# A gated linear attention with a mixture of experts on one core: one GpSimd drain is added in the last expert's first layer

## The chip, the cores and the metric

The kernel runs on one core of one Trainium2 chip. The time is the device time of one execution in microseconds; lower is better.

## What is computed

The attention part keeps a 48 x 48 state for each of 4 batches and 8 heads and steps it through 768 tokens; its output, 3072 tokens of 384 numbers, is the input of a mixture of eight experts, of which each token uses one:

```python
for t in range(S):
    state = alpha[:, :, t, :, None] * state + np.einsum('bhd,bhe->bhde', k[:, :, t], v[:, :, t])
    y[:, :, t] = np.einsum('bhd,bhde->bhe', q[:, :, t], state)
...
    h = np.maximum(x[b, s] @ w1[e], 0.0)
    out[b, s] = p[e] * (h @ w2[e])
```

The expert `e` of a token is the argmax of eight logits, or the expert of the token before it where a second gate says so; `p[e]` is the softmax weight. The inner width of an expert is 1024.

## The kernel before

The program first computes the attention in 24 blocks of 128 tokens (batch by batch within each slice of time). Beside it, routing builds for every expert a list of its tokens. The first expert is worked off in two jobs, `a` and `b`, partly beside the attention. The other seven experts are ordered by their number of tokens, and each is a job of its own, `r0` to `r6`, with as many tiles of tokens as its rank is given in `RANKS` (the last one, `r6`, has 128 + 128 + 112 rows).

A job has these steps. `gather` (line 237) fetches the rows of its tokens from DRAM with one indirect DMA on GpSimd for each tile. `trans` (line 248) transposes them on TensorE and splits them into a high and a low part. `gemm1` (line 261), the first layer, goes through eight slices `f` of the inner width: nine matmuls each into one of three PSUM tiles (`halves`, line 868), then a relu on ScalarE into `hh` and a subtraction on VectorE into `hl`. `gemm2` (line 284), the second layer, makes 24 matmuls for each tile of tokens. `store` (line 324) scales the result by the softmax weight on VectorE and sends it to its places in the output with an indirect DMA on GpSimd.

The main loop is `for n, j in enumerate(jobs)` at line 1073, with `nx` the job behind `j`. During `gemm1` of a job, GpSimd gathers the rows of `nx`, and weights of this job and the next are split by `piece` (line 1077): ScalarE makes the high part, VectorE the low part, GpSimd that of one w1 piece of a rank. In the last job, `r6`, there is no `nx`: nothing is gathered, and only the pieces 5 and 6 of its own weights, of w2, are split at `f` = 0 and 1, on ScalarE and VectorE.

The order of the instructions on each engine is the written one: every call of an engine goes through a wrapper (`Engine`, line 87, `call` at line 96) that pins it behind the call before it. Therefore nearly all rows of the profile carry line 97, the wrapper's. SyncE's queue loads the inputs and weights; GpSimd's queue has the gathers, the stores, and some elementwise work of the attention.

Behind the loop stands a branch for overflow, `with tc.If(NT > 0)` at line 1146 (`NT` is loaded at line 1144): tokens that did not fit into the tiles of their rank. With these inputs it is not taken, and each engine runs only the events that close it. Line 1303 is the line at which the program's closing barrier is made, line 1300 that of its opening one; both contain a DRAIN on every engine.

Of the kernel before, what the change touches and what calls it, by code (L numbers as in the profile page):

```python
# [72 lines left out]
def gla_moe(ctx, tc, akq, vw, vn, wg, w1, w2, cst, tok, out):  # L73
# [30 lines left out]
    v_, s_, g_, t_, y_ = (Engine(e) for e in (nc.vector, nc.scalar, nc.gpsimd, nc.tensor, nc.sync))  # L104
# [31 lines left out]
    def cc(k, p0=0, p1=128):  # L136
        a, b = _off[k]
        return cs[p0:p1, a:b]
# [928 lines left out]
    def spread(k, n):  # L1067
        return [(t + 1) * n // (k + 1) for t in range(k)]
# [4 lines left out]
    for n, j in enumerate(jobs):  # L1073
        nx = jobs[n + 1] if n + 1 < len(jobs) else None
        W, Wn = Ws[n], Ws[n + 1] if nx else None

        def piece(w, p):
            w.split(p)
            if len(w.raw) < 7:
                w.load()  # L1080
            elif n + 2 < len(Ws) and w is Wn:
                Ws[n + 2].load()
            elif Wn is not None and w is W:
                Wn.load()

        if nx:
            if n:
                nx.numbers()
            gt = nx.gather()
        for f, _ in enumerate(j.gemm1(W)):  # L1090
            if n == 1 and f == 4:
                nt = mp.tile([8, 1], F32, bufs=1, name="nt")
                gr = mp.tile([8, NOV], F32, bufs=1, name="gr")
                v_.tensor_tensor(gr, cntp.broadcast_to([8, NOV]), cc("jt", 0, 8), ALU.is_gt)
                v_.tensor_reduce(nt, gr, AX.X, ALU.add)
            if n and f < 2:
                piece(W, 5 + f)
            if n == 0 and f == 1:
                ct = pp.tile([8, 2, 128], F32, tag="xp", name="ct")
                t_.transpose(ct[:, 0], rest[:, 0], ident)  # L1100
                t_.transpose(ct[:, 1], rest[:, 1], ident)
                v_.tensor_copy(capp, ct[:, 0, 0:1])
                v_.scalar_tensor_tensor(cntp, ct[:, 1, 0:1], HALF, cc("base", 0, 8), ALU.add, ALU.subtract)
            if n == 0 and f == 2:
                for put in kept:
                    put()
            if nx:
                if 1 <= f:
                    next(gt, None)
                if n and f in (3, 5, 7):  # L1110
                    piece(Wn, (f - 3) // 2)
                if n == 0 and f % 2:
                    piece(Wn, f // 2)
            if j.thin and 2 <= f < 6:
                W.again(f - 2)
        if n == 1:
            pc.close()
            qp = ctx.enter_context(tc.tile_pool(name="qp", bufs=1, space=PSUM))

            def whole(j):  # L1120
                return lambda s, P=None: qp.tile([P or j.ways[s].stop - j.ways[s].start, DM], F32, tag="yp", bufs=3, name=f"yp_{j.nm}_{s}")
            for m in jobs[1:]:
                m.y, m.tpt = whole(m), ((pp, "xp"), (qp, "tp"))
        at_ = spread(nx.ns, 4 * j.ns - 3 * j.thin) if nx else []
        tr = nx.trans() if nx else None
        for q, _ in enumerate(j.gemm2(W)):
            if n == 1 and q == 3:
                tp = qp.tile([8, 2], F32, tag="tp", name="ovt")
                t_.matmul(tp[:, 0:1], lhsT=cc("tri8", 0, 8), rhs=nt, start=True, stop=True)
                t_.matmul(tp[:, 1:2], lhsT=cc("ones", 0, 8)[:, 0:8], rhs=nt, start=True, stop=True)  # L1130
                cum = mp.tile([8, 2], F32, bufs=1, name="cum")
                v_.tensor_copy(cum, tp)
                ti = mp.tile([8, 1], I32, bufs=1, name="ti")
                v_.tensor_copy(ti, cum[:, 1:2])
            if nx and q == 2 or nx and n and q == 0:
                piece(Wn, 3 + q // 2)
            for _ in range(at_.count(q)):
                next(tr)
        for _ in tr or ():
            pass  # L1140
# [166 lines left out]
```

## Time and profile before

| what | value |
|---|---|
| runs | 394.98, 393.0, 394.84 us, median 394.84 us |
| profiled execution | 392.89 us, span 391.1 us |
| instructions | 11445 |
| mean granted clock | 0.992 |
| TensorE busy | 95% of the span |
| VectorE, ScalarE, GpSimd busy | 64%, 45%, 43% |

The span goes from the first to the last instruction of the core. The time of an execution also holds what lies around the span, 1.8 us here. The busy times count only what an engine itself executes; waiting, branching, semaphore events and drains are done by the engine's sequencer (written with a q behind the engine's name) and are not counted.

### The profile page before, as it was taken

To read this page: it belongs to the slowest core of one execution; us is meant where nothing else is said; L and a number is where in the kernel's file an instruction comes from. 1 tells how busy PE (TensorE), PEld (TensorE's weight loads), DVE (VectorE), ACT (ScalarE), POOL (GpSimd) and SP (SyncE) were. 2 spreads that over 40 slices of the span, in tenths; PEclk is the share of its full clock that TensorE was granted. 3 is DMA by queue.
4 is the path that set the end of the run, shared out by engine and by line. 5 is a ranking of instruction groups with operands and counts; after the bars stand their busy time and mean duration, and the time that the engine had idled before them with its cause. 6 is when DMAs were issued, how large, how long until landed. Compare 5 with 4: busy or idle time off the path is not lost.

```text
span 391.1 us, 11445 instructions
## 1 busy us (share of the span) xinstructions
PE 370.5 (95%) x4536; PEld 340.9 (87%) x4536; DVE 248.5 (64%) x565; ACT 177.9 (45%) x452; POOL 166.4 (43%) x226
## 2 busy tenths in 40 slices
PE   7989988989999999999999999999999999999990
PEld 7878877878878899998899899999899899999990
DVE  8999989999875476755643562554554764564310
ACT  2476767787766530534521541542362461643200
POOL 7559666756677123344323612532522432612020
PEclk9999999999999999999999999999999999999996
DMA  8998899876746101784451572484286274561010
GB/s 235 230 246 218 234 265 261 255 208 187 208 116 180 41 2 38 226 273 151 134 163 45 153 224 78 129 293 176 100 255 251 74 236 134 158 189 59 1 42 7
DMA packets 27002, 63.30 MB, mean 162 GB/s; under 512 B 4964, under 2 KB 11446, under 8 KB 26946
## 3 DMA queue, kind: packets, MB, share of 16 engines
q1 hardware_dynamic: 23218, 52.37, 46.3%
q0 software_dynamic: 3584, 10.04, 7.4%
q8 instruction: 36, 0.59, 0.6%
q14 instruction: 20, 0.16, 0.1%
q10 hardware_dynamic: 144, 0.14, 0.1%
HBM read 53.09 MB, written 10.04 MB: 161 GB/s over the span
## 4 chain that ended last, share of the span: by engine, by line
PE 64%; DVE 15%; issue 12%; DMA 3%; POOL 2%; ACT 2%; SPq 0%; DVEq 0%; POOLq 0%; ACTq 0%
PE h_r L97 20%; PE yp_r L97 19%; PE py L97 5%; DVE sf L97 4%; DVE A L97 4%; PE pz L97 3%; DMA ld<-akq 2%; PE yp_b L97 2%; PE tp_r L97 2%; PE up L97 2%; PE h_a L97 2%; DVE pq L97 2%; POOL out L97 2%; PE yp_a L97 1%; DVE st L97 1%
## 5 line engine op out<-in xcount | busy, mean ns | idle before, releaser
L97 POOL DMA_INDIRECT out<-yo_r,ix_r x25 | 24.9, 996 | 123.4 <-DVE yo_r L97 99.1
L97 PE MATMUL yp_r<-w2h_r,hh_r 128*128 128x384 f32 (+2 forms) x184 | 63.5, 345 | 0.0
L97 PE MATMUL yp_r<-w2h_r,hl_r 128*128 128x384 f32 (+2 forms) x184 | 61.8, 336 | 0.0
L97 PE MATMUL yp_r<-w2l_r,hh_r 128*128 128x384 f32 (+2 forms) x184 | 61.6, 335 | 0.0
L97 PE MATMUL h_r<-xh_r,w1h_r 128*128 128x384 f32 (+5 forms) x168 | 59.6, 355 | 0.0
L97 PE MATMUL h_r<-xl_r,w1h_r 128*128 128x384 f32 (+5 forms) x168 | 59.4, 354 | 0.0
L97 PE MATMUL h_r<-xh_r,w1l_r 128*128 128x384 f32 (+5 forms) x168 | 59.3, 353 | 0.0
L97 DVE SCALAR_TENSOR_TENSOR hl_r<-h_r,hh_r 128x384 fp32r<-128x384 f32 (+3 forms) x56 | 32.8, 585 | 39.5 <-ACT hh_r L97 39.0
L97 ACT ACTIVATE hh_r<-h_r 128x384 fp32r<-128x384 f32 (+3 forms) x56 | 28.7, 513 | 42.8 <-PE h_r L97 42.6
L97 DVE TENSOR_TENSOR_SCAN sf<-ld,sf,zp 112x128 f32<-112x128 f32 x96 | 38.3, 462 | 0.9
L97 PEld LDWEIGHTS yp_r<-w2h_r,hh_r 128*128 128x128 f32 (+2 forms) x184 | 34.1, 186 | 0.3
L97 PEld LDWEIGHTS yp_r<-w2l_r,hh_r 128*128 128x128 f32 (+2 forms) x184 | 34.2, 186 | 0.3
L97 POOL TENSOR_TENSOR ld<-ld,sf 112x512 f32<-112x512 f32 x24 | 28.4, 1183 | 13.9 <-DVE sf L97 13.3
L97 PEld LDWEIGHTS yp_r<-w2h_r,hl_r 128*128 128x128 f32 (+2 forms) x184 | 34.1, 185 | 0.2
L97 PEld LDWEIGHTS h_r<-xh_r,w1h_r 128*128 128x128 f32 x168 | 31.5, 188 | 3.0 <-issue 1.2
L97 POOL TENSOR_TENSOR ld<-ld,A 112x512 f32<-112x512 f32 x24 | 28.4, 1183 | 13.4 <-DVE A L97 7.3
L97 PEld LDWEIGHTS h_r<-xl_r,w1h_r 128*128 128x128 f32 x168 | 31.5, 188 | 2.1 <-DVE xl_r L97 0.3
L97 PEld LDWEIGHTS h_r<-xh_r,w1l_r 128*128 128x128 f32 x168 | 31.5, 188 | 1.8
L97 ACT CAST xh_r<-tp_r 128x384 fp32r<-128x384 f32 (+4 forms) x25 | 11.4, 456 | 47.0 <-PE tp_r L97 45.9
L97 DVE TENSOR_TENSOR_SCAN A<-ld,zp 112x260 f32<-112x260 f32 x48 | 30.8, 683 | 2.7
L97 POOL DMA_INDIRECT xg_r<-xd,ix_r x25 | 28.7, 1148 | 8.6 <-issue 5.7
L97 DVE TENSOR_TENSOR xl_r<-tp_r,xh_r 128x384 fp32r<-128x384 f32 (+4 forms) x25 | 13.1, 525 | 28.1 <-ACT xh_r L97 28.1
(217 smaller groups left out, 778.6 us busy)
## 6 DMA issues: line engine op xcount, KB each, us to landing
rw_r<-w SPq DMA_DIRECT2D x21, 512.0 KB, 4.0
rw_r<-w SPq DMA_DIRECT2D x28, 384.0 KB, 4.3
ld<-akq SPq DMA_DIRECT2D x44, 192.0 KB, 4.7
vt<-vn SPq DMA_DIRECT2D x24, 192.0 KB, 4.0
xd<-XR SPq DMA_DIRECT2D x24, 192.0 KB, 3.9
ld<-akq SPq DMA_DIRECT2D x44, 97.7 KB, 4.5
wf_r<-w SPq DMA_DIRECT2D x8, 384.0 KB, 5.1
rw_a<-w SPq DMA_DIRECT2D x3, 512.0 KB, 5.0
```

The costliest lines, as they stand in the source:

```text
L97: r = f(*a, **k)
```

## The change

A call of `drain` on GpSimd is added to the main loop. It is made once, in the last job (`not nx`), when the second slice (`f == 1`) of its first layer has been written. It goes through the same wrapper as the other calls, so on GpSimd it stands behind the last store of `r5` and ahead of the first store of `r6`.

```diff
@@ -1095,6 +1095,8 @@
                 v_.tensor_reduce(nt, gr, AX.X, ALU.add)
             if n and f < 2:
                 piece(W, 5 + f)
+            if not nx and f == 1:
+                g_.drain()
             if n == 0 and f == 1:
                 ct = pp.tile([8, 2, 128], F32, tag="xp", name="ct")
                 t_.transpose(ct[:, 0], rest[:, 0], ident)
```

## Rows read from the trace of the kernel before

**Rows 1.** The page: span, and TensorE's busy time, share and instructions.
```profile
span 391.1 us, 11445 instructions
...
PE 370.5 (95%) x4536; PEld 340.9 (87%) x4536; DVE 248.5 (64%) x565; ACT 177.9 (45%) x452; POOL 166.4 (43%) x226
```

**Rows 2.** Windows: busy us of each engine from the last matmul to the end.
```profile
core 0: us, PE busy (x) PEld busy (x) DVE busy (x) ACT busy (x) POOL busy (x), PEclk, DMA share, GB/s
381.40:391.10 9.70, 0.33 (x2) 0.00 (x0) 0.62 (x1) 0.00 (x0) 0.96 (x1) 0.67 0.02 7
```

**Rows 3.** Timeline of GpSimd, last stores: start, us, what, idle before and its releaser.
```profile
358.14 0.98 POOL L97 DMA_INDIRECT out<-yo_r,ix_r  x1 [3.47 <-DVE yo_r L97]
374.33 0.98 POOL L97 DMA_INDIRECT out<-yo_r,ix_r  x1 [15.21 <-DVE yo_r L97]
378.50 0.98 POOL L97 DMA_INDIRECT out<-yo_r,ix_r  x1 [3.18 <-DVE yo_r L97]
382.66 0.96 POOL L97 DMA_INDIRECT out<-yo_r,ix_r  x1 [3.18 <-DVE yo_r L97]
```

**Rows 4.** Timeline of all engines, from 381 us on.
```profile
381.39 0.34 PE L97 MATMUL yp_r<-w2h_r,hl_r 128*112 128x384 f32 x1
381.77 0.62 DVE L97 TENSOR_SCALAR yo_r<-yp_r,pr 112x384 f32<-112x384 f32 x1 [3.54 <-PE yp_r L97]
```

**Rows 5.** Source line 1146, GpSimd: duration in ns (min/median/max), first and last start.
```profile
L1146 POOLq INC_SWDGE_SEM  x1: 1354/1354/1354, 384.1 to 384.1; - x1
```

**Rows 6.** Source line 1303: GpSimd and SyncE, whole and in windows around 385.4, 386 and 390.3.
```profile
L1303 POOLq DRAIN  x3: 46/107/4811, 385.4 to 390.8; - x3
L1303 DVEq DRAIN  x2: 10/14/17, 383.2 to 390.5; - x2
...
L1303 POOLq DRAIN  x1: 4811/4811/4811, 385.4 to 385.4; - x1
...
L1303 SPq EVENT_SEMAPHORE  x12: 28/28/28, 385.4 to 386.0; - x12
L1303 SPq DRAIN  x2: 7/10/13, 386.1 to 386.2; - x2
...
L1303 POOLq EVENT_SEMAPHORE  x2: 17/17/17, 390.3 to 390.4; - x2
```

**Rows 7.** DMA issues of GpSimd (xcount, median us to landing); packets after 384.9 us.
```profile
xg_r<-xd,ix_r POOLq DMA_INDIRECT x25, 4.3
out<-yo_r,ix_r POOLq DMA_INDIRECT x25, 2.6
...
xg_a<-xd,ix_a POOLq DMA_INDIRECT x2, 3.3
xg_b<-xd,ix_b POOLq DMA_INDIRECT x2, 3.0
out<-yo_a,ix_a POOLq DMA_INDIRECT x2, 4.4
out<-yo_b,ix_b POOLq DMA_INDIRECT x2, 3.7
...
DMA packets 0, 0.00 MB, mean 0 GB/s; under 512 B 0, under 2 KB 0, under 8 KB 0
```

**Rows 8.** Source line 1300, GpSimd: the drain of the opening barrier.
```profile
L1300 POOLq DRAIN  x1: 178/178/178, 0.3 to 0.3; - x1
```

**Rows 9.** Timelines of GpSimd, VectorE and TensorE: a subtraction beside GpSimd, and the last job's.
```profile
339.06 2.40 POOL L97 TENSOR_TENSOR w1l_r<-rw_r,w1h_r 128x1024 fp32r<-128x1024 f32 x1 [1.62 <-issue]
...
339.58 0.56 DVE L97 SCALAR_TENSOR_TENSOR hl_r<-h_r,hh_r 128x384 fp32r<-128x384 f32 x1 [1.00 <-ACT hh_r L97]
...
359.27 0.54 DVE L97 SCALAR_TENSOR_TENSOR hl_r<-h_r,hh_r 128x368 fp32r<-128x368 f32 x1 [1.41 <-ACT hh_r L97]
...
361.56 0.33 PE L97 MATMUL h_r<-xh_r,w1h_r 128*128 128x368 f32 x1
```

## The prediction, made before the changed kernel ran

> **What bounds the kernel now.** I read the page's engine shares first, then the windows, then GpSimd's timeline, and last the sequencer rows of the lines that close the program, because the shares alone do not show where this change acts. TensorE is busy for 370.5 us of a 391.1 us span [rows 1], so almost everywhere time is set by matmuls. The exception is the end: from 381.4 to 391.1 us, 9.7 us, TensorE works 0.33 us, VectorE 0.62 and GpSimd 0.96 [rows 2]. The last matmul begins at 381.39 us, VectorE scales the result at 381.77, GpSimd issues the last store at 382.66 and is done issuing at 383.62 [rows 3, 4]. The remaining 7.5 us hold no engine work at all; they belong to sequencers, which the busy rows leave out.
>
> What fills them can be read from the lines that close the overflow branch and the program. GpSimd's sequencer runs an INC_SWDGE_SEM of 1.354 us from 384.1 [rows 5], then a DRAIN from 385.4 that lasts 4.811 us, and only at 390.3 the two semaphore events with which it releases the other engines [rows 6]. SyncE has meanwhile waited through twelve events, from 385.4 to 386.0, and its own DRAIN of the closing barrier stands at 386.2 [rows 6]. VectorE's first drain of that line stands at 383.2 [rows 6], and TensorE and ScalarE have been done for longer. So from 386.2 to 390.3 everybody waits for one GpSimd drain.
>
> Is that drain waiting for data? The store issued at 382.66 takes about 2.6 us to land (the median of its kind) [rows 7], which gives 385.3, and after 384.9 no DMA packet moves at all [rows 7]. The drain starts after that. It is therefore busy with something other than the transfer. Its two neighbours are the clue: the same line shows three GpSimd drains of 46, 107 and 4811 ns [rows 6], and the one at the program's start took 178 ns [rows 8]. The long one is the only one with GpSimd's DMAs behind it: 25 + 25 + 2 + 2 + 2 + 2 = 58 indirect DMAs [rows 7], gathers and stores. 4811 / 58 = 83 ns for each. I read it as a walk over every GpSimd DMA since the last drain, landed or not; this is a reading of four numbers, not something the trace shows directly.
>
> **The change, part by part.** One instruction is added to GpSimd's stream, in the written order, after the last store of rank 5 and ahead of the first store of rank 6. Nothing is removed or moved, and SP's queue is untouched.
>
> *The new drain itself.* The store ahead of it is issued from 358.14 to 359.12 us, the first one behind it at 374.33 [rows 3]. Landing of the store ahead: 358.14 + 2.6 = 360.7 us. Its price is unknown; the nearest rows are 0.046 us (a drain with nothing to do) and 4.811 us (one over 58 DMAs) [rows 6]. I take 55 x 0.083 = 4.6 us, nearest to the second, since 55 of the 58 DMAs are older than it. If the walk begins only after landing it ends at 360.7 + 4.6 = 365.3 us; GpSimd is then idle for 9 more us. The cover is GpSimd's idle time of 15.21 us before 374.33 [rows 3]; if it were gone, the whole 4.6 us would delay rank 6's first store, and so the ones behind it. Queued behind the drain are only the three stores and the closing sequence; no other engine waits for GpSimd there, because the last rank has no gathers and its two late weight splits run on ScalarE and VectorE. Cost on the path: 0.
>
> *The closing drain.* It now has three DMAs behind it instead of 58: 3 x 0.083 = 0.25 us, in place of 4.81. Bounds: 0.046 us and 4.811 us. I add the 0.178 us of the start's drain as a base [rows 8], 0.43 us in all, so it would end at 385.4 + 0.4 = 385.9.
>
> *What is late next.* Not GpSimd any more but SyncE, whose drain stands at 386.2 [rows 6]. Its twelve waits begin when INC_SWDGE_SEM ends, 384.1 + 1.35 = 385.4, and that one ends with the last store's landing, which the change does not move. So GpSimd's event moves from 390.3 to 386.2: a gain of 4.1 us, not of the drain's 4.4.
>
> The sum: 0 - 4.1 us. Against the profiled execution, 392.89 us with a span of 391.1, that is 388.8. The three runs shown have a median of 394.84, 1.95 us above the profiled one, although their lowest, 393.0, lies close to it; I carry the difference over: 394.84 - 4.1 = **390.7 us**, 1.0% faster.
>
> **One rule weighed.** All drains of SyncE and the 46 ns one of GpSimd are short; GpSimd's at 385.4 is four hundred times longer than SyncE's median of 10 ns [rows 6]. The Trainium skill, VectorE: DVE Perf Modes, section "The DRAIN you can't avoid", says that the drains of a program's preamble and postamble take a constant 12 ns or so on all five engines. By that the added drain would cost nothing and give nothing, and the sum would be 394.8 us. The 4811 ns row contradicts it for GpSimd.
>
> **The rivals.**
> - *The closing drain's length is its own* (chance 0.11). It may be a fixed price of the first drain after DMA work, or a drain may not shorten the list that the next one walks. Then nothing changes: 394.8 us. For it: only one long drain is on record, so no scaling is shown. Against it: of the two drains of the same line that follow, neither is over 107 ns, so a drain does leave the next one little to do. To this rival belongs an added drain that skips GpSimd's DMAs. The page's rule above gives the same time.
> - *Only part is given back* (0.07). If older DMAs are dropped from the list on the way, as others reuse their places, the 4.8 us belong to fewer DMAs and the last three weigh more. With a list of 10, each costs 0.48 us and three cost 1.44: the drain would end at 385.4 + 1.44 = 386.9, a gain of 3.4 us, 391.4 us. With 6 left, 2.4 us: the gain is 2.4 and the time 392.4.
> - *VectorE is held up* (0.04), the slower side. If the drain keeps VectorE off SBUF while it walks, the place is hl of the last rank's first layer, due at 359.27 for 0.54 us [rows 9]. Three PSUM tiles serve h, so the fourth group of nine matmuls, at 361.56, waits for that hl to be done [rows 9]: 361.56 - 359.81 = 1.75 us of slack. A hold until 359.2 + 4.6 = 363.8 ends hl at 364.3, 2.8 us late on TensorE. If the closing drain stays long, the sum is 394.84 + 2.8 = 397.6 us. Against it: a real GpSimd operation of 2.40 us at 339.06 runs across an hl that starts at 339.58 and still takes 0.56 us [rows 9]. The Trainium skill, SBUF — State Buffer, section "Who interferes with whom", has an exclusive lock between GpSimd and VectorE only for VectorE instructions with two SBUF inputs or in a two-port mode; the hl row, with one input from PSUM, agrees.
>
> **How the numbers follow.** The forecast has a chance of 0.78, the rivals 0.11, 0.07 and 0.04. About 0.5%, 2.0 us here, can be told from no change. Faster by more: the forecast and the partial case, 0.85. Same: the first rival, 0.11. Slower: 0.04. The range starts at the lowest of the runs shown less the sum, 393.0 - 4.1 = 388.9, less another 0.4 for closing events that shift with the shorter drain: 388.5. It reaches up over the partial case with six DMAs to 392.5, and leaves out no change and slower, 0.15 together, and what the partial case has above that.
>
> **What would show it.** In the changed profile a GpSimd DRAIN of the kernel's wrapper line should stand between 359 and 366 us with about 4.6 us, GpSimd's stores of rank 6 at the same distance from the last matmuls as now, and the closing drain well under 1 us, with the span at about 387.0. A closing drain still near 4.8 us proves the first rival; one between 1 and 3 us the second; hh or hl rows that slide past 361.56 the third. If the closing drain is short and the end still comes late, SyncE's twelve events or the INC_SWDGE_SEM have grown, and the step "late next" is the wrong one.

## The result and the profile after

The changed kernel took 389.95, 389.84, 390.67 and 388.01 us, median 389.89, beside a median of 393.92 us for four runs of the kernel before. The ratio of the changed kernel to the one before is 0.9854 (95% interval 0.981 to 0.9898); it is not formed from these two medians, whose quotient is 0.990. In a second series with more runs the ratio is 0.9905 (0.9874 to 0.9937). The two intervals overlap from 0.9874 to 0.9898; the kernel is faster by about 1%, as forecast (390.7 us, range 388.5 to 392.5).

The profiled execution took 389.95 us with a span of 388.1. The second of these windows of the kernel after, from its last matmul on, answers to [rows 2], GpSimd's timeline to [rows 3], the timeline of all engines to [rows 4]; the first window is that of the added drain:

```profile
core 0: us, PE busy (x) PEld busy (x) DVE busy (x) ACT busy (x) POOL busy (x), PEclk, DMA share, GB/s
...
359.00:365.00 6.00, 6.00 (x38) 6.00 (x37) 3.45 (x7) 3.36 (x6) 0.98 (x1) 1.00 0.07 27
382.60:388.10 5.50, 0.36 (x3) 0.02 (x1) 0.62 (x1) 0.00 (x0) 0.96 (x1) 0.91 0.04 12
...
359.36 0.98 POOL L97 DMA_INDIRECT out<-yo_r,ix_r  x1 [3.47 <-DVE yo_r L97]
375.56 0.98 POOL L97 DMA_INDIRECT out<-yo_r,ix_r  x1 [15.21 <-DVE yo_r L97]
379.73 0.98 POOL L97 DMA_INDIRECT out<-yo_r,ix_r  x1 [3.18 <-DVE yo_r L97]
383.89 0.96 POOL L97 DMA_INDIRECT out<-yo_r,ix_r  x1 [3.17 <-DVE yo_r L97]
...
382.62 0.34 PE L97 MATMUL yp_r<-w2h_r,hl_r 128*112 128x384 f32 x1
383.00 0.62 DVE L97 TENSOR_SCALAR yo_r<-yp_r,pr 112x384 f32<-112x384 f32 x1 [3.54 <-PE yp_r L97]
```

Up to the last store nothing is nearer or farther than before: the store still comes 1.27 us after the last matmul's start (382.62 to 383.89; before 381.39 to 382.66), and GpSimd's idle time ahead of rank 6's stores is 15.21, 3.18 and 3.17 us, within 0.01 us of [rows 3]. What shrank is the part behind: from the last store's start to the end of the span 388.1 - 383.9 = 4.2 us, before 391.1 - 382.7 = 8.4 us. The span fell by only 3.0 us, because this execution reached its last matmul 1.2 us later than the one profiled before; it is already 0.9 us later at the first gather of job `a`, at 115.9 us instead of 115.0, more than 200 us ahead of the added drain, and the whole 1.2 us later at the store just ahead of that drain (359.36 against 358.14). That is the scatter of the body from one execution to the next, not the change.

The sequencer rows of the kernel after (lines 97, 1148 and 1305 answer to the wrapper's line 97 and to lines 1146 and 1303 of before) show where the 4.2 us went; the last line is the time that the last store took to land:

```profile
L97 POOLq DRAIN  x1: 5790/5790/5790, 359.1 to 359.1; - x1
...
L1148 POOLq INC_SWDGE_SEM  x1: 254/254/254, 385.3 to 385.3; - x1
...
L1305 POOLq DRAIN  x3: 46/107/1146, 385.6 to 387.8; - x3
...
L1305 SPq EVENT_SEMAPHORE  x12: 28/28/961, 385.5 to 387.1; - x12
L1305 SPq DRAIN  x2: 7/10/13, 387.2 to 387.2; - x2
...
L1305 POOLq EVENT_SEMAPHORE  x2: 17/17/17, 387.3 to 387.3; - x2
...
DMA to landing us min/median/max: 2.7/2.7/2.7
```

Four things stand in these rows. The added drain stands on the sequencer from 359.1 to 364.9 us, and the issue of the store ahead of it (359.36 to 360.35) lies inside that row, so behind the issue it takes 4.57 us; TensorE is busy throughout (6.00 of 6 us from 359 to 365). The closing drain fell from 4811 to 1146 ns. INC_SWDGE_SEM, an instruction of GpSimd's sequencer in the closing of the overflow branch, fell from 1354 to 254 ns, which the prediction had not expected. And one of SyncE's twelve events, all of 28 ns before, now takes 961 ns and ends at 386.6: SyncE waits there for the landing of the last store (383.9 + 2.7). GpSimd's releasing events follow SyncE's drain, 387.3 after 387.2; GpSimd's own drain ended at 385.6 + 1.1 = 386.7.

### The profile page after: what moved, and what is told of

The parts are those of the page before. It is cut to its first block, busy times and chain, and to the rows that moved or that the text cites. A ratio compares the mean times of both kernels' runs of the same rounds, so it can differ in the third digit from the quotient of the medians.

```text
span 388.1 us, 11446 instructions
## 1 busy us (share of the span) xinstructions
PE 371.4 (96%) x4536; PEld 341.8 (88%) x4536; DVE 248.7 (64%) x565; ACT 178.0 (46%) x452; POOL 166.7 (43%) x226
## 4 chain that ended last, share of the span: by engine, by line
PE 62%; DVE 16%; issue 14%; DMA 3%; POOL 2%; ACT 1%; POOLq 0%; DVEq 0%; SPq 0%; ACTq 0%
PE h_r L97 20%; PE yp_r L97 20%; DVE sf L97 5%; DVE A L97 4%; PE py L97 4%; PE pz L97 4%; PE h_a L97 2%; PE tp_r L97 2%; PE up L97 2%; DVE pq L97 2%; DVE st L97 2%; PE yp_a L97 1%; POOL out L97 1%; DMA xg_r<-xd,ix_r 1%; PE lq L97 1%
```

## The experiments

**The changed kernel again.** No edit; more rounds.

> The changed kernel itself, timed in more rounds. The closing part, from the start of the last store to the end of the span, took 8.4 us before and 4.2 us after in the two profiles, so the theory that the whole gain is the shorter closing drain (walk theory: about 83 ns for each GpSimd DMA since the last GpSimd drain) expects 4.0 to 4.4 us less than the kernel before, a ratio of 0.989 to 0.990. A second gain somewhere in the body, which the ratio of 0.985 with its interval of 0.981 to 0.990 leaves room for, would show as a ratio below 0.987.

Measured: ratio 0.9905 (0.9874 to 0.9937), median 390.03 against 394.9 us. The medians are 4.9 us apart, the ratio stands for 3.8 us, and the 4.2 us of the closing part lie between. From the last store to the end of the span it took 4.1 us. The interval holds the gain of the closing part, about 4.2 / 394.9 = 1.1%, and the ratio gives no sign of a second one. Why the first series gave 0.985 is not shown; its own medians give 0.990.

**The drain where nothing hides it.**

```diff
+    g_.drain()
     pinned[0] = False
     NT = nc.values_load(...
```

(without the call in the loop)

> The same drain, but written behind the last store of the last rank, so that nothing hides it. Walk theory: it visits all 58 DMAs where it stands, 58 x 83 ns = 4.8 us from 383.6, and the closing drain then only waits for nothing or little (under 0.3 us); the span ends within 0.5 us of the kernel before, 391 us. Rival (an added drain makes the closing one cheap at no price of its own): about 4 us faster, as the change was.

Sequencer rows of this kernel, the added drain, INC_SWDGE_SEM, the closing drains, and the load of `NT` on GpSimd; the last line is the same load in the kernel before:

```profile
L97 POOLq DRAIN  x1: 6008/6008/6008, 382.8 to 382.8; - x1
...
L1147 POOLq INC_SWDGE_SEM  x1: 195/195/195, 390.5 to 390.5; - x1
...
L1304 POOLq DRAIN  x3: 34/51/107, 390.7 to 392.0; - x3
...
L1145 POOLq TENSOR_LOAD <-ti x1: 503/503/503, 389.3 to 389.3; - x1
...
L1144 POOLq TENSOR_LOAD <-ti x1: 505/505/505, 382.8 to 382.8; - x1
```

The last store is issued from 383.06 to 384.02 and the drain ends at 388.8, 4.8 us behind it. The first of the closing drains, the one that took 4811 ns before, takes 51 ns. The time is that of the kernel before, 0.9985 (0.9958 to 1.0011). The span, though, ended at 392.3 us and not within 0.5 us of 391: its part behind the last store took 9.2 us, 0.8 more than before. The load of `NT` and the branch, which GpSimd's sequencer ran beside the last store before, wait for the drain here. So a drain does not make the work cheaper, it does it earlier; the change gains because it does it beside matmuls.

**A drain of another engine.**

```diff
             if not nx and f == 1:
-                g_.drain()
+                v_.drain()
```

> The added drain is one of VectorE at the same place of the program, none of GpSimd. Walk theory: nothing changes, the closing GpSimd drain stays at 4.7 to 4.9 us and the ratio is 0.997 to 1.003. Rival (any added instruction shifts what follows, such as the loading of code, and the gain comes from that): a ratio near 0.99.

```profile
L97 DVEq DRAIN  x1: 997/997/997, 361.8 to 361.8; - x1
...
L1305 POOLq DRAIN  x1: 4811/4811/4811, 385.8 to 385.8; - x1
```

Ratio 1.0006 (0.9974 to 1.0039), and the closing GpSimd drain has the very 4811 ns of [rows 6]. (The 997 ns of VectorE's drain hold the 0.96 us split of w2 that begins with it.) This shifts the code of VectorE alone, not GpSimd's; that a shift of GpSimd's code is not the cause either is shown further on, where the same GpSimd drain, put elsewhere, leaves closing drains of 1605 and 3483 ns.

**The drain where its cover is short.**

```diff
         for q, _ in enumerate(j.gemm2(W)):
+            if not nx and q == 8:
+                g_.drain()
```

(without the call in `gemm1`)

> The GpSimd drain stands between the second and the third store of the last rank, where GpSimd has about 3.2 us to spare. Walk theory: it visits 57 DMAs, 57 x 83 ns = 4.7 us from the end of the second store's issue (379.5 us in the profile before), so until 384.2; the last store, otherwise at 382.7, starts some 1.7 us later, and the end is 1.7 us later than in the changed kernel: a gain of some 2.5 us, a ratio of 0.993 to 0.995. Rival (an added drain is free wherever it stands): a gain of 4 us.

GpSimd's and VectorE's timelines of this kernel, last tile, and its closing rows:

```profile
382.85 0.98 POOL L97 DMA_INDIRECT out<-yo_r,ix_r  x1 [3.18 <-DVE yo_r L97]
389.47 0.96 POOL L97 DMA_INDIRECT out<-yo_r,ix_r  x1 [5.64 <-issue]
...
386.12 0.62 DVE L97 TENSOR_SCALAR yo_r<-yp_r,pr 112x384 f32<-112x384 f32 x1 [3.54 <-PE yp_r L97]
...
L1148 POOLq INC_SWDGE_SEM  x1: 209/209/209, 390.9 to 390.9; - x1
...
L1305 POOLq DRAIN  x1: 1061/1061/1061, 391.1 to 391.1; - x1
```

The ratio is 0.9929 (0.9897 to 0.9961): the gain is smaller than with the drain in its cover, though the intervals of the two overlap. The trace is clearer. The drain's row (5950 ns from 382.6) ends at 388.6, 4.7 us behind the second store's issue. The last store's data were ready at 386.74, and without the drain the store would have begun 0.27 us later, as in [rows 3, 4]: 387.0. It begins at 389.47, 2.5 us late, where 1.7 were expected; behind the drain's end 0.9 us more go by until the issue begins, which the walk does not include. So by the trace the gain left is 8.4 - (2.5 + 4.1) = 1.8 us, with the 4.1 us behind the last store, and not the expected 2.5; the ratio stands for 2.8. This profiled execution is one of the long ones of its series (395.41 us, median 391.86), in part for what is told at the end.

**Another number of DMAs on the list.** In two kernels the only drain stands earlier, in a third the kernel before has more DMAs:

```diff
+            if n == 4 and f == 7:
+                g_.drain()
...
+            if n == 1 and f == 7:
+                g_.drain()
...
+            if n and f > 4:
+                g_.dma_start(scr[:, 3 * (n - 1) + f - 5], cst[0:16, 0:4])
```

> The drain is moved to the last slice of the first layer of the fourth ranked expert; 39 GpSimd DMAs stand ahead of it and 19 behind. Walk theory (83 ns for each DMA since the last GpSimd drain): 39 x 83 ns = 3.2 us there; the closing drain takes 19 x 83 ns = 1.6 us, and INC_SWDGE_SEM, which fell from 1.354 us with 58 DMAs to 0.254 with 3 and 0.195 with none, takes 0.195 + 19 x 0.020 = 0.58 us. Rival (the first drain behind DMA work pays a fixed price of 4.7 us): 4.7 us in the middle, and the closing one ends with the landing of the last store, about 1.1 us, as in the changed kernel.

> The drain is moved to the last slice of the first layer of the first ranked expert; 16 GpSimd DMAs stand ahead of it and 42 behind. Walk theory: closing drain 42 x 83 ns = 3.5 us, INC_SWDGE_SEM 0.195 + 42 x 0.020 = 1.04 us. Fixed-price rival: a closing drain of about 1.1 us and INC_SWDGE_SEM of 0.25 us.

> The kernel before, without any added drain, and with 21 more GpSimd DMAs that carry 256 bytes each (three in each ranked expert's first layer, into a scratch tile that nothing reads). Walk theory by DMAs: the closing drain goes through 79 instead of 58, 79 x 83 ns = 6.6 us, and INC_SWDGE_SEM takes 0.195 + 79 x 0.020 = 1.8 us. Rival (the walk is over rows or bytes): the closing drain stays at 4.8 to 4.9 us. Fixed-price rival: 4.8 us.

Closing rows of the three kernels, in this order; for the first also the added drain and the GpSimd work ahead of it:

```profile
285.84 2.39 POOL L97 TENSOR_TENSOR w1l_r<-rw_r,w1h_r 128x1024 fp32r<-128x1024 f32 x1 [1.83 <-ACT w1h_r L97]
...
L97 POOLq DRAIN  x1: 5718/5718/5718, 285.8 to 285.8; - x1
...
L1148 POOLq INC_SWDGE_SEM  x1: 574/574/574, 385.0 to 385.0; - x1
...
L1305 POOLq DRAIN  x1: 1605/1605/1605, 385.6 to 385.6; - x1
```

```profile
L1148 POOLq INC_SWDGE_SEM  x1: 1034/1034/1034, 385.3 to 385.3; - x1
...
L1305 POOLq DRAIN  x1: 3483/3483/3483, 386.4 to 386.4; - x1
```

```profile
L1149 POOLq INC_SWDGE_SEM  x1: 1801/1801/1801, 385.5 to 385.5; - x1
...
L1306 POOLq DRAIN  x3: 46/103/6526, 387.3 to 394.4; - x3
```

Put in order of the GpSimd DMAs issued since the last GpSimd drain:

| kernel | DMAs | INC_SWDGE_SEM, ns | closing drain, ns |
|---|---|---|---|
| drain behind the last store | 0 | 195 | 51 |
| drain before the last store | 1 | 209 | 1061, waits for the landing |
| changed kernel | 3 | 254 | 1146, waits for the landing |
| drain in the fourth ranked expert | 19 | 574 | 1605 |
| drain in the first ranked expert | 42 | 1034 | 3483 |
| kernel before | 58 | 1354 | 4811 |
| kernel before, 21 small DMAs more | 79 | 1801 | 6526 |

Where the drain does not wait for a landing, it is a straight line: (6526 - 1605) / 60 = 82 ns for each DMA, 83 to 84 from zero. The added drain of the fourth ranked expert fits as well: with 39 DMAs it ended at 291.5 us, 3.3 us behind the work ahead of it (285.84 + 2.39 = 288.23), where the walk wanted 3.2 and a fixed price 4.7. INC_SWDGE_SEM follows another: (1801 - 195) / 79 = 20 ns for each. The small DMAs carry 256 bytes each, the others up to 192 KB; the price goes by DMAs, not by bytes or rows. A fixed price of the first drain is excluded. In the one execution of each kernel the spans were 388.0 (19 DMAs), 390.7 (42) and 394.7 us (79).

**Is the list cleared?** The drain of the fourth ranked expert and that of the change together, and the same with the first one in the fifth ranked expert:

```diff
+            if (n == 4 and f == 7) or (not nx and f == 1):
+                g_.drain()
...
+            if (n == 5 and f == 7) or (not nx and f == 1):
+                g_.drain()
```

> Both drains: the one of the fourth ranked expert and the one of the change. Walk theory: the second finds 16 DMAs, 16 x 83 ns = 1.3 us behind the end of the last issue, so it ends with the landing of that store, about 1.6 us behind its issue, where it ended 4.57 us behind it in the changed kernel; the closing drain is as in the changed kernel. Rival (a drain goes through all GpSimd DMAs of the program again): the second still ends 4.6 us behind the issue.

The second drain ended 2.2 us behind the issue (3413 ns from 363.3, the issue ending at 364.53). That is far from the 4.6 us of a walk over everything, so a drain clears the list for the next one; but the walk theory, as written, wanted 1.6. The store landed at 366.0, 2.5 us after its start, and the drain ended 0.7 us behind that. In the closing drains with 3 DMAs and with 1 the same distance was 0.17 and 0.08 us. A second theory, two passes of 41 ns for each DMA with the wait between them, was put against a single pass:

> As the run with two drains, but the first stands in the fifth ranked expert, so that the second finds 9 DMAs. There the second drain ended 0.70 us behind the landing of the store ahead of it with 16 DMAs on the list, and the closing ones 0.17 us behind it with 3 and 0.08 with 1. Two-pass theory (each pass 41 ns for a DMA; the first passes over the list and waits for the last landing, the second follows it): 9 x 41 ns = 0.37 us and 0.04, so 0.4 us behind the landing. One-pass theory (83 ns each, then the wait for the last one): 0.1 us behind the landing, and the 0.70 us was a disturbance.

> The run with two drains once more. Two-pass theory: the second drain ends 0.65 to 0.75 us behind the landing again. One-pass theory: 0.1 us behind it.

The second drain of either kernel and the store ahead of it, first with 9 DMAs, then with 16 again:

```profile
L97 POOLq DRAIN  x1: 3126/3126/3126, 359.7 to 359.7; - x1
...
359.89 0.99 POOL L97 DMA_INDIRECT out<-yo_r,ix_r  x1 [3.47 <-DVE yo_r L97]
```

```profile
L97 POOLq DRAIN  x1: 3412/3412/3412, 362.3 to 362.3; - x1
...
362.52 0.98 POOL L97 DMA_INDIRECT out<-yo_r,ix_r  x1 [3.47 <-DVE yo_r L97]
```

With 2.5 us to landing, the first landed at 362.4 and the drain ended at 362.8, 0.4 us behind it; the second at 365.0 and 365.7, 0.7 us behind it again. Four points, 0.08, 0.17, 0.4 and 0.7 us for 1, 3, 9 and 16 DMAs, lie on one line of some 41 ns for each, from 0.04 us. A fifth point was on record already: the added drain of the first ranked expert, with 16 DMAs, ended 0.71 us behind the landing of the newest. About half of the 83 ns is paid only when the newest DMA has landed. That there are two passes is the simplest reading; the rows do not show the passes themselves.

**What the end waits for now.** The last tile's scaling was divided between two engines, in the changed kernel:

```diff
-            v_.tensor_scalar_mul(yo, yp, self.pr[0:P, 0, s:s + 1])
+            c = DM // 2 if self.nm == "r6" and s == 2 else DM
+            v_.tensor_scalar_mul(yo[:, 0:c], yp[:, 0:c], self.pr[0:P, 0, s:s + 1])
+            if c < DM:
+                s_.mul(yo[:, c:], yp[:, c:], self.pr[0:P, 0, s:s + 1])
```

> The changed kernel with the last tile's scaling divided: VectorE makes the left 192 columns, ScalarE the right 192, which shortens the way from the last matmul to the last store. If the landing of the last store is what the end now waits for, the time from the end of the last matmul to the end of the span falls by what the store moves forward, about 0.25 us, from 5.0 to 5.1 us to 4.75 to 4.85. If the closing drain's own walk or INC_SWDGE_SEM still set the end, it falls by the same, since these follow the store too, but the closing drain would be longer than the wait for the landing; if something else of the program's end does, it stays at 5.0 to 5.1.

```profile
388.82 0.42 DVE L97 TENSOR_SCALAR yo_r<-yp_r,pr 112x192 f32<-112x192 f32 x1 [3.54 <-PE yp_r L97]
389.27 0.42 ACT L97 ACTIVATE yo_r<-yp_r,pr 112x192 f32<-112x192 f32 x1 [12.49 <-DVE yo_r L97]
389.96 0.96 POOL L97 DMA_INDIRECT out<-yo_r,ix_r  x1 [3.43 <-ACT yo_r L97]
```

A miss: the halves share a tile, so ScalarE waited for VectorE, and they ran one behind the other; a half also costs 0.42 us, not half of 0.62. From the last matmul to the end it took 5.2 us instead of 5.0 to 5.1. The store came 0.25 us later relative to the last matmul, and the part behind it stayed at 4.0 to 4.1 us, so the end does follow the last store. The other traces tell more: in the seven executions with one or three DMAs on the closing list, the last store lands 2.54 to 2.71 us after its start, and the span ends 1.50 us behind the landing in every one. So the end waits for that landing. A version that beats the changed kernel did not come out of this.

## What the prediction had right, and the step that failed

*The long drain is a walk over GpSimd's DMAs.* Right, and its 83 ns too: 82 ns from the slope between 19 and 79 DMAs, with a row of 51 ns for none. "Landed or not" is right of the first half of the price alone: some 41 ns of it for each DMA are due only behind the newest landing.

*The added drain, 55 x 0.083 = 4.6 us, hidden.* Right: 4.57 us behind the store's issue, ended at 364.9, and GpSimd's wait of 15.21 us ahead of the next store has not changed by a hundredth. That the walk might begin only after landing is refuted: it would have ended 4.6 us behind the landing and ended 3.1 behind it.

*The closing drain, 0.43 us.* Mis-sized: it took 1.146 us. The term had three DMAs and a base, and left out that a drain with a store in flight waits for its landing; before, the landing was over when the drain began. It cost nothing on the path, since GpSimd's drain ended at 386.7 and SyncE's came at 387.2.

*INC_SWDGE_SEM ends with the last store's landing, which the change does not move.* This is the step that failed. In the profile before it ended at 385.4, just behind the landing at 385.2, and I took nearness for a cause. The runs show 20 ns for each DMA on the list plus 0.195 us: 1.354 us with 58, 0.254 with 3. In the changed kernel it ends at 385.5, 1.0 us ahead of the landing at 386.6. So the change did move this term, and SyncE's twelve events with it.

*SyncE is late next.* Right, for another reason. Its twelve events do begin when INC_SWDGE_SEM ends, now 1.1 us earlier relative to the last store, but one of them then stands 961 ns for the landing. The two differences nearly cancel: SyncE's drain came 3.5 us behind the last store's start before (386.2 - 382.7) and 3.3 us after (387.2 - 383.9). Hence 4.2 us from the closing part where the sum said 4.1. That they cancel is luck: with 58 DMAs INC_SWDGE_SEM happens to end 2.75 us behind the last store's start, and the landing comes after 2.6 to 2.7 us.

*From the sum to the time.* 390.7 forecast, 389.89 measured. The sum was set on a median of 394.84, 1.95 us above the profiled execution; with one run more the median of before is 393.92, and 393.92 - 4.1 = 389.8. By these runs the base was off, by the scatter of single executions; in the second series it is 394.9 again, with 390.03 for the changed kernel. Times do not settle here where the last 0.8 us lie.

*The signs.* The prediction said that a closing drain between 1 and 3 us would prove the partial case. It took 1.146 us, and yet the partial case is wrong: the sign did not reckon with the wait for the landing. The span was to be at about 387.0 and was 388.1, for the 1.2 us of scatter in the body.

*The rivals.* A fixed price of the closing drain fell with the table above. So did, for GpSimd, the rule of the Trainium skill, VectorE: DVE Perf Modes, section "The DRAIN you can't avoid", that such drains take some 12 ns on every engine; on the other four engines the closing drains took 7 to 17 ns, as it says. (GpSimd's is 481 times SyncE's median, not four hundred.) The partial case fell as well: the price for each DMA is the same with 19 and with 79 on the list, so none of the 58 had been dropped on the way. VectorE was not held up:

```profile
360.50 0.54 DVE L97 SCALAR_TENSOR_TENSOR hl_r<-h_r,hh_r 128x368 fp32r<-128x368 f32 x1 [1.41 <-ACT hh_r L97]
361.21 0.96 DVE L97 TENSOR_TENSOR w2l_r<-rw_r,w2h_r 128x768 fp32r<-128x768 f32 x1 [0.18 <-ACT w2h_r L97]
...
362.78 0.33 PE L97 MATMUL h_r<-xh_r,w1h_r 128*128 128x368 f32 x1
```

These rows of the kernel after stand inside the added drain. The subtraction takes the 0.54 us of [rows 9] and begins with the same wait for ScalarE; the fourth group of matmuls begins 2.28 us after it, before 361.56 - 359.27 = 2.29. Even the split of w2, with two inputs in SBUF, takes 0.96 us, as in the kernel before.

## What to carry to other kernels

Look at what the sequencers do behind the last engine work; the busy rows do not show it, and a closing GpSimd drain there cost 83 ns in this kernel for every DMA that GpSimd had issued since its last drain. A kernel with many of them can pay that early, with a drain where GpSimd is idle for longer than the walk, and here it gained the full price only then: behind the last store the same drain gave nothing, and with too little cover it held the last store up. And an instruction that ends just behind an event need not have waited for it; only a run in which the two come apart tells.

## What was not expected of the hardware

INC_SWDGE_SEM takes 20 ns for each GpSimd DMA on the list, from 195 ns with none to 1801 with 79. About half of a drain's price, 41 ns for each DMA, falls due only behind the landing of the newest one.

The body's scatter has a visible part. In the profiled execution with the drain before the last store, TensorE's granted clock stood at 0.51 of full speed, the 1.2 GHz level, from 54 to 61 us, between stretches at 2.4 GHz. Windows of that kernel:

```profile
45.00:54.00 9.00, 6.71 (x194) 5.57 (x185) 8.44 (x22) 5.99 (x20) 4.92 (x5) 1.00 0.92 260
54.00:61.00 7.00, 6.32 (x106) 5.43 (x106) 2.07 (x5) 1.98 (x5) 1.64 (x2) 0.51 0.56 148
61.00:70.00 9.00, 8.71 (x246) 7.33 (x245) 8.29 (x26) 6.68 (x24) 6.09 (x5) 1.00 0.75 235
```

In the stretch before the fall TensorE was busy for 6.71 of 9 us. The first gather of job `a` came at 119.5 us there, 3.6 us later than in the changed kernel, and the last matmul began 3.1 us later (385.7 against 382.6). The executions with two drains, and the one with the divided scaling, show such a stretch too, at other times of the attention part; the kernel before and the changed kernel, as profiled, have none. Why it comes in some executions was not tried.
